# Spectral layer and feed-forward on one core: new places for pairs, chunks and waves in the slot plan, y in two slots, the sum split a slot later, parts of the inverse matrices kept in DRAM

## The chip, the core and the metric

The program runs on one core of one Trainium2 chip. The metric is device time in microseconds, from the first to the last instruction of the program; lower is better. The engines that matter are TensorE (PE in the profile; its weight loads are PEld), VectorE (DVE), ScalarE (ACT), GpSimd (POOL) and SyncE (SP), which issues the DMAs.

## The reference

```python
X = np.fft.rfft(x, axis=1)                     # x: 8 x 3008 x 256, float32
Yr = Xr @ w_r - Xi @ w_i + b_r
Yi = Xr @ w_i + Xi @ w_r + b_i
Y  = sign(Y) * max(abs(Y) - 0.01, 0)           # both parts
y  = np.fft.irfft(Y, n=3008, axis=1)
h  = y.reshape(24064, 256) @ w_in              # 256 x 2048
out = (h - np.tanh(h)) @ w_out                 # 2048 x 256
```

## The kernel before

**The feed-forward and its slots.** The 24064 tokens are cut into 48 chunks of some 502, and the 2048 inner columns into 16 blocks of 128; one block of one chunk is a *slot*, so there are 768 slots, and 16 slots are a *band*. In slot g, TensorE first does the six "up" matmuls (L691, into h) of slot g+2, then what the plan has put into slot g, then the six "down" matmuls (L724, into the two banks o) of slot g. Each product is three matmuls, because both operands are split into a high and a low part: g = h - tanh(h) is made by ACT (th, L702) and DVE (g, L705), and split by ACT (gh, L708) and DVE (gl, L711). At a band's end ACT (L734) and DVE (L742) copy the two banks o to ot, and the next band's first "down" needs these banks.

**The spectral work in between.** The length 3008 = 64 x 47 is transformed in two steps, forward and backward, batch by batch. Batch 0 is done ahead of the slots, in an order written out by hand. For batches 1 to 7 the work lies in the slots:

- a *fold* (class Folded): DVE adds and subtracts inputs (L333), TensorE does 32 small matmuls in one go (L342) into **four** banks of PSUM's pool ps_f, and ACT and DVE write the result to the DRAM tensor a; four per batch (two for batch 1)
- a *pair* (class Both, two units of class Spectrum): 64 small matmuls (L494) into **two** banks of ps_f; `take` copies and splits the result on ACT and DVE (xh, xl, xi), and splits the sum xi (s)
- the unit's products: `cross` (L419, bank ps_v of ps_f, held until DVE has added y, L450) and `shared` (L419, bank ps_t of ps_f; DVE: tb L436, y L450 four times, mn L439 and L440)
- `matrix`: loads the unit's inverse matrix (turn) and splits it (turn_h on ACT, turn_l on DVE); `inverse` (L465 to L467, a bank ps_i of ps_f, copied to zo by ACT, L472), which is stored to the DRAM tensor z
- a *wave* (class Wave): 80 small matmuls (L654) into **two** banks of ps_f, in two halves that use different rows of the array; the results are copied to yt by ACT and DVE (L663) and split by `halves` into yh and yl, the chunk's input

**What sets the order.** Pool ps_f has four banks, and fold, pair, wave, ps_v, ps_t and ps_i share them. `plan_spectrum`, `plan_folded` and the loop over chunks put each step into a numbered slot (`put`); the instructions are then written slot by slot, and the framework's scheduler may still shift an instruction within its engine by a little. Each engine then runs its own queue strictly in that order. The plan before puts a wave into the slot of a pair, where one is near:

```python
near = range(asked[w] + 6, min(asked[w] + 11, last + 1))
slot = asked[w] + 3 if c == 2 else next((k for k in near if k in whole), near[len(near) // 2])
```

Of the kernel before, what the change touches and what calls it, by code (L numbers as in the profile page):

```python
# [10 lines left out]
F32 = mybir.dt.float32  # L11
# [3 lines left out]
ALU = mybir.AluOpType  # L15

B, S, D, FF = 8, 3008, 256, 2048
NP, NJ, KR, GB = 32, 24, 48, 5
# [77 lines left out]
def spectral_ffn(ctx, tc, x, w_r, w_i, w_in, w_out, x_fold, b_turned, f1, f1b, f1f, f2, f2f, i1, i1w, i2, out):  # L96
    nc = tc.nc
    P = 128
# [34 lines left out]
    def split(src, name, pool=const, tag=None, bufs=None, rest=nc.vector):  # L133
        hi, lo = pair_like(src, name, pool, tag, bufs)
        split_into(hi, lo, src, rest)
        return hi, lo
# [113 lines left out]
            nc.gpsimd.tensor_tensor(out=lo, in0=self.w, in1=hi.bitcast(F32), op=ALU.subtract)  # L250

    a_dram, z_dram = {}, {}
    XC = 4
    PAIRED, LOOK = 1, 4
    NEAR = 32
# [119 lines left out]
    class Spectrum:  # L375
# [20 lines left out]
        def take(self, ps):  # L396
            self.xh = work.tile([P, 2, 2, P], F32R, name="xh", tag="sp_h", bufs=3)
            self.xl = work.tile([P, 2, 2, P], F32R, name="xl", tag="sp_l", bufs=3)
            xi = work.tile([P, 2, P], F32, name="xi")
            flat, one = "p t r (j s k) -> p s (t r j) k", "p t (j s k) -> p s t j k"  # L400
            xh, xl = (x.rearrange(flat, j=2, s=2) for x in (self.xh, self.xl))
            xv = xi.rearrange(one, j=2, s=2)
            whole = [p.rearrange("p (x k) -> p x k", k=32) for p in ps]
            part = [p.rearrange("p (t r j k) -> p r t j k", t=2, r=2, j=2) for p in ps]
            for s in range(2):
                nc.scalar.copy(out=xh[:, s], in_=whole[s])  # L406
            for s in range(2):
                nc.scalar.copy(out=xv[:, s], in_=part[s][:, 1])
            for s in range(2):
                nc.vector.tensor_tensor(out=xl[:, s], in0=whole[s], in1=xh[:, s].bitcast(F32), op=ALU.subtract)  # L410
            for s in range(2):
                nc.vector.tensor_tensor(out=xv[:, s], in0=part[s][:, 0], in1=xv[:, s], op=ALU.add)  # L412
            self.s = split(xi, f"s_{self.b}_{self.jp}", work, "s")

        def product(self, dst, hi, lo, w):
            n = 0
# [10 lines left out]
                self.product(self.vv[:, D:], self.xh[:, :, 0], self.xl[:, :, 0], lin[1])  # L427

        def matrix(self):
            self.turns = split(self.turn, f"turn_{self.b}_{self.jp}", work, "turn", 2)  # L430

        def shared(self):
            t1 = ps_f.tile([P, 512], F32, name="ps_t1", tag="f")
            self.product(t1[:, :D], *self.s, lin[0])
            tb = self.temp("tb", "th")
            nc.vector.tensor_tensor(out=tb, in0=t1[:, :D].unsqueeze(1).to_broadcast([P, 2, D]), in1=bias, op=ALU.add)  # L436
            y = self.add(lambda jj, ri: tb[jj * 64:(jj + 1) * 64, ri, :])
            mn = work.tile([P, 2, D], F32, name="mn", tag="tmp", bufs=4)
            nc.vector.tensor_scalar_min(out=mn, in0=y, scalar1=-LAM)  # L439
            nc.vector.scalar_tensor_tensor(out=mn, in0=y, scalar=LAM, in1=mn, op0=ALU.max, op1=ALU.add)  # L440
            self.mn = mn
# [1 line left out]
        def halve(self):  # L443
            self.z = split(self.mn, f"z_{self.b}_{self.jp}", work, "sp", 3)

        def add(self, common):
            y = self.temp("y", "g")
            for ri in range(2):
                for jj in range(2):
                    nc.vector.tensor_tensor(  # L450
                        out=y[ri * 64:(ri + 1) * 64, jj, :], in0=common(jj, ri),
                        in1=self.side(ri)[jj * 64:(jj + 1) * 64], op=ALU.add,
                    )
            return y

        def side(self, ri):
            return self.vv[:, ri * D:(ri + 1) * D]
# [12 lines left out]
        def put(self, pz):  # L470
            zo = work.tile([P, 512], F32, name="zo", tag="tmp", bufs=4)
            nc.scalar.copy(out=zo, in_=pz)  # L472
            self.zo = zo
            self.store(0, P)
# [28 lines left out]
    class WholeSpectrum(Spectrum):  # L503
# [22 lines left out]
        def sum(self):  # L526
            pr = self.ps.rearrange("p (t r m) -> p t r m", t=2, r=2)
            self.sf = work.tile([P, 2, P], F32, name="sf", tag="s_h")
            nc.vector.tensor_tensor(out=self.sf, in0=pr[:, :, 0, :], in1=self.xf[:, :, 1, :], op=ALU.add)
# [28 lines left out]
        def common(self):  # L558
            self.tb = work.tile([P, D], F32, name="tb0", tag="xi")
            nc.scalar.copy(out=self.tb, in_=self.t1)  # L560
# [62 lines left out]
    class Wave:  # L623
# [20 lines left out]
        def time(self):  # L644
            half = self.half
            ps = [ps_f.tile([P, 512], F32, name="ps_i2", tag="f") for _ in range(2)]
            pv = [p[:, :2 * half * 47].rearrange("p (t c) -> p t c", t=2) for p in ps]
            for k in range(half):
                for t in range(2):
                    for h in range(2):  # L650
                        rows = slice(64 * h, 64 * h + KR)
                        for c in range(2):
                            at = t * P + 64 * c
                            nc.tensor.matmul(  # L654
                                pv[h][64 * c:64 * c + 64, t, 47 * k:47 * k + 47],
                                self.zt[rows, k, at:at + 64], i2t[rows, :47], start=True, stop=True,
                            )
            pool, tag = self.home
            for t in range(2):
                self.y[t] = pool.tile([P, PITCH], F32, name="yt", tag=tag)  # L660
            for h, copy in enumerate((nc.scalar.copy, nc.vector.tensor_copy)):
                for t in range(2):
                    copy(out=self.y[t][:, 47 * h * half:47 * (h + 1) * half], in_=pv[h][:, t])  # L663

# [327 lines left out]
    def put(slot, fn, *a, turn=1):  # L992
        slots.setdefault(slot, ([], [], []))[turn].append((fn, a))

    def plan_folded(b, wanted):
        last = 0
        for k, ideal in enumerate(wanted):
            f = Folded(b, k)
            spots = [g for g in range(max(last + 6, ideal - 4), ideal + 9) if all(abs(g - h) > 2 - (b == 2) for h in busy) and g not in held]
            at = min(spots, key=lambda g: abs(g - ideal) + 2 * (g % NF > 10))  # L1000
            put(max(FIXED, at - 6, last + 1), f.load)
            for i in range(4):
                put(max(FIXED, at - 4 + i), f.fold, i // 2, i % 2)
            put(at, f.dft, turn=2)
            for g in range(2):
                put(at + 1 + g, f.join, g, turn=0)
            last = at

    def plan_spectrum(units, start, each, ahead, lag, rest):
        for jp, s in enumerate(units):  # L1010
            at = start + int(jp * each)
            early = start + int((jp - jp % 2) * each)
            put(early - ahead, s.load)
            if jp % 2:
                pair = Both(units[jp - 1:jp + 1])
                put(early, pair.dft, turn=2)
                for v in range(2):
                    put(early + v, pair.take, v, turn=0 if v else 2)
                whole.add(early)
            if units is not second or jp >= 2:  # L1020
                put(at + lag - 3, s.load_turn)
                put(at + lag, s.matrix)
            put(at + lag, s.cross, 0)
            held.update((at + lag, at + lag + 1))
            put(at + lag + 1, s.cross, 1)
            put(at + lag + 2, s.shared)
            put(at + lag + 2 + rest, s.halve)
            put(at + 2 * lag + 3 + rest // 2, s.inverse)

    put(FIXED, load_second)  # L1030
    whole, held = set(), set()
    asked, new = {}, {}
    for c in range(2, NCH):
        new[c] = [w for w in chunks[c].parts if w.w > 1 and w not in asked]
        last, spaced = (9, 1) if c == 2 else (2, 4)
        for k, w in enumerate(reversed(new[c])):
            asked[w] = NF * (c - 1) + last - spaced * k
    plan_spectrum(second, 46, 2.95, 5, 2, 0)
    asked[waves[len(waves) // B]] += 4
    ends = {b: asked[waves[b * len(waves) // B]] - 2 for b in range(2, B)}  # L1040
    for b in range(2, B):
        plan_spectrum([Spectrum(b, jp) for jp in range(NJ // 2)], ends[b] - 61, 4.6, 5, 2, 2)
    busy = set(whole)
    for c in range(2, NCH):
        last = NF * (c - 1) + 12
        for w in new[c]:
            put(asked[w], w.load)
            near = range(asked[w] + 6, min(asked[w] + 11, last + 1))
            slot = asked[w] + 3 if c == 2 else next((k for k in near if k in whole), near[len(near) // 2])
            put(slot, w.time, turn=2)  # L1050
            busy.add(slot)
        for t in range(2):
            put(min(slot + 1 + t, last + 1), chunks[c].halves, t)
    plan_folded(1, (33, 39))
    plan_folded(2, (73, 79, 85, 96))
    for b in range(3, B):
        plan_folded(b, range(ends[b] - 106, ends[b] - 70, 9))
    for g in range(FIXED, len(order)):
        if g + AHEAD < len(order):
            c, f = order[g + AHEAD]  # L1060
# [50 lines left out]
```

## Time and profile before

| | |
|---|---|
| runs | 2483.96, 2479.15, 2486.25 us; median 2483.96 |
| the profiled execution | 2483.84 us, of which its span is 2482.1 us |
| mean granted TensorE clock | 0.997 |
| TensorE busy | 2460.8 us, 99% of the span |
| VectorE, ScalarE busy | 1827.0 us (74%), 1344.8 us (54%) |
| DMA | 182.73 MB, the main queue busy 25.4% of 16 engines' span |

The profiled execution lies 0.12 us under the median. A busy TensorE here does not say that it runs at its peak: matmuls overlap, and their ends are modelled. What it loses is read from the distance of the *starts* of its instructions in the timeline.

### The profile page before, as it was taken

To read this page: it belongs to the slowest core of one execution; us is meant where nothing else is said; L and a number is where in the kernel's file an instruction comes from. 1 tells how busy PE (TensorE), PEld (TensorE's weight loads), DVE (VectorE), ACT (ScalarE), POOL (GpSimd) and SP (SyncE) were. 2 spreads that over 40 slices of the span, in tenths; PEclk is the share of its full clock that TensorE was granted. 3 is DMA by queue.
4 is the path that set the end of the run, shared out by engine and by line. 5 is a ranking of instruction groups with operands and counts; after the bars stand their busy time and mean duration, and the time that the engine had idled before them with its cause. 6 is when DMAs were issued, how large, how long until landed. Compare 5 with 4: busy or idle time off the path is not lost.

```text
span 2482.1 us, 47486 instructions
## 1 busy us (share of the span) xinstructions
PE 2460.8 (99%) x19274; PEld 2147.9 (87%) x19274; DVE 1827.0 (74%) x3421; ACT 1344.8 (54%) x2755; POOL 34.5 (1%) x31
## 2 busy tenths in 40 slices
PE   9999999999999999999999999999999999999999
PEld 6798978888888898888888888889888898888888
DVE  5887887677777777777776778767786687755555
ACT  5665555555555555555555555555455555554554
POOL 2110000000000000000000000000000000000000
PEclk9999999999999999999999999999999999999999
DMA  8633134111341114311143212421124221010000
GB/s 259 184 88 109 65 97 127 46 58 47 103 105 41 63 39 112 97 56 55 39 127 81 65 51 58 114 76 53 51 65 98 59 60 44 31 50 17 24 14 17
DMA packets 121323, 182.73 MB, mean 74 GB/s; under 512 B 11985, under 2 KB 85807, under 8 KB 121104
## 3 DMA queue, kind: packets, MB, share of 16 engines
q1 hardware_dynamic: 121104, 179.70, 25.4%
q8 instruction: 151, 2.47, 0.4%
q14 instruction: 68, 0.56, 0.1%
HBM read 104.68 MB, written 74.97 MB: 72 GB/s over the span
## 4 chain that ended last, share of the span: by engine, by line
PE 88%; DVE 7%; ACT 3%; DMA 1%; issue 1%; SPq 0%; ACTq 0%; DVEq 0%
PE o L724 37%; PE h L691 36%; PE ps_v L419 4%; PE ps_i L654 3%; PE ps_t L419 2%; PE ps_f L494 1%; DVE g L705 1%; DVE y L450 1%; PE ps_f L342 1%; DVE gl L711 1%; PE ps_f L290 1%; PE ps_i L465 1%; PE ps_i L466 1%; PE ps_i L467 1%; ACT gh L708 1%
## 5 line engine op out<-in xcount | busy, mean ns | idle before, releaser
L708 ACT CAST gh<-g 128x502 fp32r<-128x502 f32 (+2 forms) x768 | 469.4, 611 | 547.5 <-DVE g L705 545.1
L711 DVE TENSOR_TENSOR gl<-g,gh 128x502 fp32r<-128x502 f32 (+2 forms) x768 | 522.0, 680 | 298.4 <-ACT gh L708 286.6
L705 DVE TENSOR_TENSOR g<-h,th 128x502 f32<-128x502 f32 (+2 forms) x768 | 520.5, 678 | 261.0 <-ACT th L702 256.6
L702 ACT ACTIVATE th<-h 128x502 f32<-128x502 f32 (+2 forms) x768 | 453.3, 590 | 441.8 <-PE h L691 437.8
L724 PE MATMUL o<-gh,wout_l 128*128 128x502 f32 (+2 forms) x1536 | 590.7, 385 | 3.5 <-ACT ot L734 2.9
L724 PE MATMUL o<-gl,wout_h 128*128 128x502 f32 (+2 forms) x1536 | 577.6, 376 | 0.0
L724 PE MATMUL o<-gh,wout_h 128*128 128x502 f32 (+2 forms) x1536 | 577.3, 376 | 0.0
L691 PE MATMUL h<-yh,win_l 128*128 128x502 f32 (+2 forms) x1536 | 452.6, 376 | 2.1 <-DVE g L705 1.3
L691 PE MATMUL h<-yl,win_h 128*128 128x502 f32 (+2 forms) x1536 | 451.6, 376 | 0.7 <-DVE yl L683 0.7
L691 PE MATMUL h<-yh,win_h 128*128 128x502 f32 (+2 forms) x1536 | 451.3, 376 | 0.0
L724 PEld LDWEIGHTS o<-gh,wout_l 128*128 128x128 f32 x1536 | 290.4, 189 | 63.4 <-ACT th L702 13.4
L691 PEld LDWEIGHTS h<-yh,win_l 128*128 128x128 f32 x1536 | 289.8, 189 | 40.0 <-DVE g L705 2.1
L691 PEld LDWEIGHTS h<-yl,win_h 128*128 128x128 f32 x1536 | 290.7, 189 | 36.7 <-DVE yl L683 2.2
L724 PEld LDWEIGHTS o<-gl,wout_h 128*128 128x128 f32 x1536 | 290.5, 189 | 36.6 <-DVE gl L711 1.2
L691 PEld LDWEIGHTS h<-yh,win_h 128*128 128x128 f32 x1536 | 291.1, 190 | 34.7
L724 PEld LDWEIGHTS o<-gh,wout_h 128*128 128x128 f32 x1536 | 290.9, 189 | 27.6 <-issue 0.8
L450 DVE TENSOR_TENSOR y<-tb,ps_v 64x256 f32<-64x256 f32 x336 | 140.1, 417 | 3.4
L682 ACT CAST yh<-yt 128x470 fp32r<-128x470 f32 (+38 forms) x200 | 83.0, 460 | 24.5 <-PE h L691 15.9
L683 DVE TENSOR_TENSOR yl<-yt,yh 128x470 fp32r<-128x470 f32 (+38 forms) x200 | 78.5, 420 | 16.1 <-ACT yh L682 14.8
L654 PEld LDWEIGHTS ps_i<-i,zin 48*64 48x64 f32 x4096 | 72.6, 137 | 19.5 <-issue 11.9
L654 PE MATMUL ps_i<-i,zin 48*64 48x47 f32 x4096 | 79.7, 235 | 3.7 <-DVE w_f L245 1.5
L406 ACT CAST xh<-ps_f 128x256 fp32r<-128x256 f32 x168 | 58.8, 374 | 43.0 <-DVE xi L412 42.8
(116 smaller groups left out, 2210.5 us busy)
## 6 DMA issues: line engine op xcount, KB each, us to landing
xt<-in_x_fold SPq DMA_DIRECT2D x52, 512.0 KB
at<-a SPq DMA_DIRECT2D x96, 256.0 KB
z<-zo SPq DMA_DIRECT2D x92, 256.0 KB
zin<-z SPq DMA_DIRECT2D x92, 240.0 KB
a<-st SPq DMA_DIRECT2D x216, 96.0 KB
out<-ot SPq DMA_DIRECT2D x29, 502.0 KB
turn<-in_i SPq DMA_DIRECT2D x84, 128.0 KB
out<-ot SPq DMA_DIRECT2D x16, 504.0 KB
```

The source lines that it names most:

```text
L406: nc.scalar.copy(out=xh[:, s], in_=whole[s])
L419: nc.tensor.matmul(paired(dst, D), lhs[:, t], in_turn(rhs[:, t, :]), start=n == 0, stop=n == 5)
L450: nc.vector.tensor_tensor(out=y[ri * 64:(ri + 1) * 64, jj, :], in0=common(jj, ri), in1=self.side(ri)[jj * 64:(jj + 1) * 64], op=ALU.add,)
L654: nc.tensor.matmul(pv[h][64 * c:64 * c + 64, t, 47 * k:47 * k + 47], self.zt[rows, k, at:at + 64], i2t[rows, :47], start=True, stop=True,)
L682: nc.scalar.copy(out=yh, in_=y)
L683: nc.vector.tensor_tensor(out=yl, in0=y, in1=yh.bitcast(F32), op=ALU.subtract)
L691: nc.tensor.matmul(paired(h, n), lhs[:, t, f * P:(f + 1) * P], moving(rhs[:, t], n), start=k == 0, stop=k == 5,)
L702: nc.scalar.activation(out=th[:, :n], in_=h[:, :n], func=AF.Tanh)
L705: nc.vector.tensor_tensor(out=g[:, :n], in0=h[:, :n], in1=th[:, :n], op=ALU.subtract)
L708: nc.scalar.copy(out=gh[:, :n], in_=g[:, :n])
L711: nc.vector.tensor_tensor(out=gl[:, :n], in0=g[:, :n], in1=gh[:, :n].bitcast(F32), op=ALU.subtract)
L724: nc.tensor.matmul(paired(self.o[t], n), lhs[:, f, t * P:(t + 1) * P], in_turn(rhs[:, :n]), start=f == 0 and k == 0, stop=f == NF - 1 and ...
```

## The change

All places are now chosen by new rules. A pair is moved off the last two slots of a band (`clear`) and planned together with its two units (`plan_pair`); a wave goes, within its five slots, to the one farthest from pairs, folds and other waves; a fold is kept out of the slots from a unit's products to its threshold (`held`) and pays for each slot that it is nearer than 3 to another burst. For batches 2 to 7 y is added in two slots instead of one. The split of the sum is a step of its own, a slot later than `take`. The split inverse matrices of batch 1 are written to DRAM, and batches 2 to 7 load both parts from there, into the tiles that the splits wrote before. For all batches but 0, ACT makes all four copies yt of a wave. The arithmetic is the same, and so is the number of TensorE's instructions of each kind.

```diff
 def take(self, ps):
...
-            self.s = split(xi, f"s_{self.b}_{self.jp}", work, "s")
+            self.xi = xi
+
+        def sum(self):
+            self.s = split(self.xi, f"s_{self.b}_{self.jp}", work, "s")
...
         def matrix(self):
+            if self.b > PAIRED:
+                self.turns = pair_like(i1[:, :2], f"turn_{self.b}_{self.jp}", work, "turn", 2)
+                for k, t in enumerate(self.turns):
+                    nc.sync.dma_start(out=t.bitcast(F32), in_=turns_dram[self.jp, k])
+                return
             self.turns = split(self.turn, f"turn_{self.b}_{self.jp}", work, "turn", 2)
+            for k, t in enumerate(self.turns):
+                nc.sync.dma_start(out=turns_dram[self.jp, k], in_=t.bitcast(F32))
...
-            for h, copy in enumerate((nc.scalar.copy, nc.vector.tensor_copy)):
+            for h in range(2):
+                copy = nc.scalar.copy if h == 0 or self.b else nc.vector.tensor_copy
...
+    def away(g):
+        return min(abs(g - h) for h in busy)
...
-            spots = [g for g in range(max(last + 6, ideal - 4), ideal + 9) if all(abs(g - h) > 2 - (b == 2) for h in busy) and g not in held]
-            at = min(spots, key=lambda g: abs(g - ideal) + 2 * (g % NF > 10))
+            spots = [g for g in range(max(last + 6, ideal - 4), ideal + 9) if g not in held]
+            at = min(spots, key=lambda g: abs(g - ideal) + 2 * (g % NF > 10) + 5 * max(0, 3 - away(g)))
...
+    def plan_pair(units, at, apart, calm):
+        pair = Both(units)
+        put(at, pair.dft, turn=2)
+        busy.add(at)
+        for v, s in enumerate(units):
+            put(at - 5, s.load)
+            put(at + v, pair.take, v, turn=0 if v else 2)
+            put(at + 1 + v, s.sum)
+            g = at + v * apart + 2
+            if s.b > PAIRED or s.jp >= 2:
+                if s.b == PAIRED:
+                    put(g - 3, s.load_turn)
+                put(g, s.matrix)
+            for k in range(2):
+                put(g + k, s.cross, k)
+            held.update(range(g, g + 2 + 2 * calm))
+            put(g + 2, s.shared)
+            put(g + 2 + calm, s.threshold)
+            put(g + 2 + 2 * calm, s.halve)
+            put(g + 5 + calm, s.inverse)
+
+    def clear(g):
+        while g % NF in (14, 15):
+            g += 1 if g % NF == 15 else -1
+        return g
...
-            slot = asked[w] + 3 if c == 2 else next((k for k in near if k in whole), near[len(near) // 2])
+            slot = asked[w] + 3 if c == 2 else max(near, key=lambda g: min(4, away(g)))
```

**Where it shows in the order: a fold.** TensorE's queue, first fold of the batch that starts near slot 166; `ps_t` is the unit's last product, `ps_f...<-e` the fold. Before:

```order
L419 MATMUL ps_t_7588<-w_h,s_10_h 128x256 x2
L724 MATMUL o_7377<-gh,wout_l 128x502
L724 MATMUL o_7377<-gh,wout_h 128x502
L724 MATMUL o_7377<-gl,wout_h 128x502
L724 MATMUL o_7378<-gh,wout_l 128x502
L724 MATMUL o_7378<-gh,wout_h 128x502
L724 MATMUL o_7378<-gl,wout_h 128x502
L691 MATMUL h<-yh,win_l 128x502 x2
L691 MATMUL h<-yh,win_h 128x502 x2
L691 MATMUL h<-yl,win_h 128x502 x2
L342 MATMUL ps_f_7629<-e,f1f 32x512
L342 MATMUL ps_f_7630<-e,f1f 32x512
```

In the changed kernel the same fold stands in slot 173, four slots behind the last product, and right behind that unit's inverse (`ps_i`):

```order
L705 MATMUL h<-yh,win_l 128x502 x2
L705 MATMUL h<-yh,win_h 128x502 x2
L705 MATMUL h<-yl,win_h 128x502 x2
L478 MATMUL ps_i_7861<-z_11_l,turn_11_h 128x256
L479 MATMUL ps_i_7861<-z_11_h,turn_11_l 128x256
L480 MATMUL ps_i_7861<-z_11_h,turn_11_h 128x256
L478 MATMUL ps_i_7861<-z_11_l,turn_11_h 128x256
L479 MATMUL ps_i_7861<-z_11_h,turn_11_l 128x256
L480 MATMUL ps_i_7861<-z_11_h,turn_11_h 128x256
L343 MATMUL ps_f_7873<-e,f1f 32x512
L343 MATMUL ps_f_7874<-e,f1f 32x512
```

The fold moved from one slot behind a product to four slots behind it, and an inverse moved in front of it.

**A wave.** TensorE's queue in slot 522 before: the end of a pair (`ps_f...<-...at`), then the wave (`ps_i...<-...zin`), cut in two by the scheduler:

```order
L494 MATMUL ps_f_20997<-f_135,at 64x2x32 x2
L494 MATMUL ps_f_20998<-f_135,at 64x2x32 x2
L654 MATMUL ps_i_21046<-i_259,zin 64x47 x20
L724 MATMUL o_20614<-gh,wout_l 128x504
L724 MATMUL o_20614<-gh,wout_h 128x504
L654 MATMUL ps_i_21047<-i_259,zin 64x47 x20
L724 MATMUL o_20614<-gl,wout_h 128x504
L724 MATMUL o_20615<-gh,wout_l 128x504
```

A wave of the changed kernel, in slot 508; the nearest pair stands four slots ahead, in slot 504, and the wave follows an inverse and a unit's last product:

```order
L480 MATMUL ps_i_20308<-z_1_h,turn_1_h 128x256
L423 MATMUL ps_t_20318<-w_h,s_2_l 128x256 x2
L423 MATMUL ps_t_20318<-w_l,s_2_h 128x256 x2
L423 MATMUL ps_t_20318<-w_h,s_2_h 128x256 x2
L667 MATMUL ps_i_20334<-i_260,zin 64x47 x2
L667 MATMUL ps_i_20335<-i_260,zin 64x47 x2
L667 MATMUL ps_i_20334<-i_260,zin 64x47 x2
```

Pair and wave moved apart, the wave is whole, and its two halves alternate again; an inverse and a product stand in front of it instead.

**A band's end.** DVE's queue at the end of the band in front of slot 160 in the changed kernel (at the same band end before, `ot` stands ahead of `tb` and of all four `y`):

```order
L719 TENSOR_TENSOR g<-h,th 128x502
L447 TENSOR_TENSOR tb<-ps_t_7333,bias 128x512
L725 TENSOR_TENSOR gl<-g,gh 128x502
L465 TENSOR_TENSOR y<-tb,ps_v 64x256 x2
L756 COPY ot<-o_6730 128x504
L465 TENSOR_TENSOR y<-tb,ps_v 64x256 x2
L719 TENSOR_TENSOR g<-h,th 128x502
```

Here tb and two of the y moved in front of the copy ot.

## Rows read from the trace of the kernel before

**Rows 1.** Timeline of PE: a fold alone; columns: start us, length us, instruction.
```profile
666.39 0.63 PE L342 MATMUL ps_f<-e,f1f 24*32 24x512 f32 x4
...
667.46 0.48 PE L724 MATMUL o<-gh,wout_l 128*128 128x502 f32 x1
667.77 0.38 PE L724 MATMUL o<-gh,wout_h 128*128 128x502 f32 x1
667.99 0.38 PE L724 MATMUL o<-gl,wout_h 128*128 128x502 f32 x1
```

**Rows 2.** Timeline of PE: a fold one slot behind a product; in brackets: idle, releaser.
```profile
1842.10 1.05 PE L342 MATMUL ps_f<-e,f1f 24*32 24x512 f32 x6
1843.41 0.61 PE L342 MATMUL ps_f<-e,f1f 24*32 24x512 f32 x1 [0.25 <-DVE y L450]
...
1844.47 0.48 PE L724 MATMUL o<-gh,wout_l 128*128 128x502 f32 x1
```

**Rows 3.** Timeline of all engines: a fold right behind an inverse.
```profile
377.46 1.36 PE L342 MATMUL ps_f<-e,f1f 24*32 24x512 f32 x7
377.57 0.59 ACT L472 COPY zo<-ps_i 128x512 f32<-128x512 f32 x1
...
379.27 0.48 PE L724 MATMUL o<-gh,wout_l 128*128 128x502 f32 x1
```

**Rows 4.** Timeline of PE: a fold cut in two around three "down" matmuls.
```profile
327.06 1.47 PE L342 MATMUL ps_f<-e,f1f 24*32 24x512 f32 x5
...
331.45 0.48 PE L724 MATMUL o<-gh,wout_l 128*128 128x502 f32 x1
```

**Rows 5.** Timeline of PE: a wave alone, a pair alone, a pair with a wave.
```profile
425.53 1.38 PE L654 MATMUL ps_i<-i,zin 48*64 48x47 f32 x80
426.84 0.48 PE L724 MATMUL o<-gh,wout_l 128*128 128x504 f32 x1
...
461.66 1.16 PE L494 MATMUL ps_f<-f,at 64*64 64x64 f32 x64
462.75 0.48 PE L724 MATMUL o<-gh,wout_l 128*128 128x502 f32 x1
...
490.52 1.16 PE L494 MATMUL ps_f<-f,at 64*64 64x64 f32 x64
...
492.78 0.48 PE L724 MATMUL o<-gh,wout_l 128*128 128x502 f32 x1
```

**Rows 6.** Timeline of PE: product, pair and a wave cut in two, around two "downs".
```profile
1451.58 1.16 PE L494 MATMUL ps_f<-f,at 64*64 64x64 f32 x64
1453.03 1.37 PE L654 MATMUL ps_i<-i,zin 48*64 48x47 f32 x40 [0.29 <-DVE tb L436]
...
1456.72 0.48 PE L724 MATMUL o<-gl,wout_h 128*128 128x504 f32 x1
```

**Rows 7.** Busy time by stretch: us, PE, PEld, DVE, ACT, POOL, granted clock, DMA, GB/s.
```profile
1758.90:1766.00 7.10, 7.05 (x52) 6.04 (x53) 3.99 (x12) 2.15 (x8) 0.00 (x0) 0.52 0.10 30
...
2066.40:2069.80 3.40, 3.40 (x14) 2.73 (x11) 2.79 (x9) 1.80 (x6) 0.00 (x0) 0.50 0.22 58
```

**Rows 8.** Timeline of PE: first "down" matmuls of a band, at two band ends.
```profile
559.71 0.39 PE L419 MATMUL ps_v<-w_h,xh 128*128 128x256 f32 x2
561.05 0.48 PE L724 MATMUL o<-gh,wout_l 128*128 128x504 f32 x1 [0.96 <-ACT ot L734]
...
1626.33 0.48 PE L724 MATMUL o<-gh,wout_l 128*128 128x502 f32 x1 [0.22 <-DVE ot L742]
```

**Rows 9.** Timeline of PE: first "up" matmuls of a chunk whose wave came late.
```profile
1103.74 0.69 PE L691 MATMUL h<-yl,win_h 128*128 128x504 f32 x2 [0.49 <-DVE yl L683]
```

**Rows 10.** Groups by line: count, then busy us, mean ns, idle before and releaser.
```profile
L143 DVE TENSOR_TENSOR turn_l<-turn,turn_h 128x256 fp32r<-128x256 f32 x84 | 36.2, 431 | 7.5 <-ACT turn_h L142 7.1
L663 ACT COPY yt<-ps_i 128x235 f32<-128x235 f32 (+1 forms) x112 | 32.4, 341 | 3.3 <-PE ps_i L654 3.2
```

**Rows 11.** The chain that ended last: start us, us, what; the slowest landing in it.
```profile
969.94 6.58 DMA xt<-in_x_fold
```

More of the change, by code (lines that the diff above doesn't have):

```diff
@@ L252, in spectral_ffn @@
     a_dram, z_dram = {}, {}
+    turns_dram = dram.tile([NJ // 2, 2, P, 2, P], F32, name="turns", bufs=1)
     XC = 4
@@ L434, in shared, with threshold @@
             self.product(t1[:, :D], *self.s, lin[0])
-            tb = self.temp("tb", "th")
+            tb = self.tb = self.temp("tb", "th")
             nc.vector.tensor_tensor(out=tb, in0=t1[:, :D].unsqueeze(1).to_broadcast([P, 2, D]), in1=bias, op=ALU.add)
-            y = self.add(lambda jj, ri: tb[jj * 64:(jj + 1) * 64, ri, :])
+            self.y = self.temp("y", "g")
+            self.add(0)
+        def threshold(self):
+            y = self.y
+            self.add(1)
             mn = work.tile([P, 2, D], F32, name="mn", tag="tmp", bufs=4)
@@ L444, in halve, with add @@
             self.z = split(self.mn, f"z_{self.b}_{self.jp}", work, "sp", 3)
[L446 to L454, printed above, removed]
+        def add(self, ri):
+            for jj in range(2):
+                rows = slice(jj * 64, jj * 64 + 64)
+                nc.vector.tensor_tensor(
+                    out=self.y[ri * 64:(ri + 1) * 64, jj, :], in0=self.tb[rows, ri, :], in1=self.side(ri)[rows], op=ALU.add,
+                )
         def side(self, ri):
@@ L1006, in plan_folded @@
                 put(at + 1 + g, f.join, g, turn=0)
+            busy.add(at)
             last = at
[L1009 to L1028, printed above, removed]
+    def plan_pair(units, at, apart, calm):
+        pair = Both(units)
+        put(at, pair.dft, turn=2)
+        busy.add(at)
+        for v, s in enumerate(units):
[18 more added lines that the diff above has]
+        return g
     put(FIXED, load_second)
-    whole, held = set(), set()
+    busy, held = set(), set()
     asked, new = {}, {}
@@ L1037, in spectral_ffn @@
             asked[w] = NF * (c - 1) + last - spaced * k
-    plan_spectrum(second, 46, 2.95, 5, 2, 0)
+    for jp in range(0, NJ // 2, 2):
+        plan_pair(second[jp:jp + 2], 46 + int(jp * 2.95), 3, False)
     asked[waves[len(waves) // B]] += 4
@@ L1041, in spectral_ffn @@
     for b in range(2, B):
-        plan_spectrum([Spectrum(b, jp) for jp in range(NJ // 2)], ends[b] - 61, 4.6, 5, 2, 2)
-    busy = set(whole)
+        units = [Spectrum(b, jp) for jp in range(NJ // 2)]
+        for jp in range(0, NJ // 2, 2):
+            plan_pair(units[jp:jp + 2], clear(ends[b] - 61 + int(jp * 4.6)), 4, True)
+    busy |= {27, 28}
+    plan_folded(1, (33, 39))
+    plan_folded(2, (84, 90, 97, 103))
+    for b in range(3, B):
+        plan_folded(b, range(ends[b] - 99, ends[b] - 72, 8))
     for c in range(2, NCH):
@@ L1053, in spectral_ffn @@
             put(min(slot + 1 + t, last + 1), chunks[c].halves, t)
[L1054 to L1057, printed above, removed]
     for g in range(FIXED, len(order)):
```

## The prediction

> **What bounds the kernel now.** The first part of the page has TensorE busy almost throughout, so I looked for what TensorE does in that time, in the timeline of PE. In a slot without extra work a matmul starts every 0.21 us [rows 1], 12 of them make 2.54 us, and a burst of small matmuls stands between "up" and "down" at a price of its own: 1.07 us for a fold (666.39 to 667.46), 1.09 for a pair, 1.31 for a wave [rows 1, 5]. Leaving a burst costs 0.10 us more (the first "down" takes 0.31 instead of 0.21 [rows 1]); entering one costs the same, so 0.20 together. Most slots of the trace run at exactly these prices. VectorE and ScalarE have room on average, so only places count where TensorE's starts are farther apart. I went through all slots for such places, and then asked the chain of waits and the brackets of the timeline who ended each wait. Nearly all of them are waits for a PSUM bank, or bursts that got in each other's way. So the gain can be no more than the sum of these places, and each is asked: is it still there in the new order?
>
> **The change part by part.**
>
> *Folds.* A fold needs all four banks of ps_f. Before there are 26. Of these 17 cost 1.07 us. Four stand one slot behind a product, and wait until DVE has added y and so released ps_v: 1842.10 to 1844.47, 2.37 us, 1.30 too much [rows 2]. Two stand right behind an inverse and wait for the copy zo: 1.81 us, 0.74 too much [rows 3]. Three stand in the slot of the product itself, and the scheduler cut them in two: 4.39 us from 327.06 to 331.45, less three "downs" (0.64) and the 1.07: 2.68 too much [rows 4]; I take 2.68 for all three. Sum 5.2 + 1.5 + 8.0 = 14.7 us. In the new order none is cut, none stands nearer than two slots behind a product (a slot is 2.54 us, more than the 1.30 that is late now), but four stand right behind an inverse, as in [rows 3]: 4 x 0.74 = 3.0 stays. **-11.7 us.**
>
> *Pairs and waves.* Before, 11 waves follow a pair in its slot. Six are whole: 490.52 to 492.78, 2.26 us, where pair and wave alone cost 1.09 + 1.31 + 0.20 = 2.60; moving them apart costs 6 x 0.34 = 2.0. Three stand behind a product and a pair, and find no bank: the wave waits for tb, then for y, is cut in two, and each half takes as long as a whole wave (1.30), since its two halves no longer alternate. 1451.58 to 1456.72 is 5.14 us, less two "downs" (0.42): 4.72, 2.12 too much [rows 6], times three 6.4. Two more are cut in batch 1, one of their halves without a wait; half the price, 1.06 each. In the new order no wave is cut or follows a pair. -(6.4 + 2.1 - 2.0) = **-6.5 us.**
>
> *Clock.* Behind two of the three cut waves the granted clock falls to 1.2 GHz: 0.52 over 7.1 us and 0.50 over 3.4 us [rows 7], that is 7.1 x 0.48 + 3.4 x 0.50 = 5.1 us lost. Just before, TensorE had done a pair and a cut wave with three waits. Elsewhere, delayed folds included, the clock is 1.00. As this pattern is gone: **-5.1 us.**
>
> *New neighbours.* In nine slots a pair (six) or a wave (three) now follows an inverse and a product, with a bank to wait for that zo's copy releases. In [rows 3] the bank comes 0.74 us late to a burst right behind the inverse; here a product lies between, six matmuls of half the columns, 6 x 0.11 = 0.67 us. Bounds 0 and 0.74 each; I take 0.1, nearest to the covered case: **+0.9 us** (at most 6.7).
>
> *Band ends.* Before, three band ends with a product and `take` at the same place wait for ACT's copy ot: due 0.22 us after 559.71, come at 561.05, 1.12 late, 3.4 in all; eleven more are late by 0.1 to 0.5 us, as at 1626.33 (0.22 in the bracket, and 0.16 that the modelled end of the matmul before hides, as in the other one: 1.12 against 0.96) [rows 8], some 3.3 in all. New: `clear` moves pairs away, but four band ends have a fold's additions ahead of DVE's copy, as that one, three have tb and two y ahead of it (some 1.7 us, at 0.43 for 256 columns on DVE [rows 10]), one has tb and four, and the ones with xl and xi stay similar. I take 0.4 for each of the first eight and 0.25 for seven others, 5.0 instead of 6.7: **-1.7 us** (bounds -6.7, and +3 if the new ones cost as much as the old worst).
>
> *Late waves.* Before, at three chunk starts the "up" matmuls wait for yh and yl, since the wave stood behind a pair late in the band: the bracket has 0.49 us for the worst wait [rows 9]; with the shorter ones at the same starts some 0.9 each, 2.7. In the new order waves of such a kind are earlier, or whole and alone; three late ones behind a product stay, with yl fewer instructions back in DVE's queue; 0.3 each. **-1.8 us.**
>
> *Inverse matrices and yt.* 72 splits leave DVE (0.431 us, 31 us in all) and ACT (about as much), and 98 copies yt move to ACT (0.341 us, 33 us) [rows 10]. No wait of TensorE is put down to them, so they are worth 0 on the path beyond the places above. DMA grows by 72 x 128 KB of loads and 24 x 128 KB of stores: 0, hidden, since a load has six slots, over 15 us, until its inverse, and the slowest landing in the chain took 6.58 us [rows 11]. If that cover were gone, see the first rival. y in two slots holds ps_v a slot longer; in the new order nobody asks for that bank in this slot. The later split of the sum puts four products of batch 1 (before two) into the middle of the "down" matmuls, and waits that an order can't show will come: **+2.5 us** (0 to 6).
>
> Sum: -11.7 - 6.5 - 5.1 + 0.9 - 1.7 - 1.8 + 2.5 = -23.4. From the profiled execution, 2483.84: **2460.4 us**; the median of the runs lies 0.12 above, so 2460.
>
> **A rule that speaks against it.** The Trainium skill (TensorEngine Tiling (Array Packing), section Tiling Modes) says that changing the tiling mode, not just the tile, drains TensorE. Fold, pair and wave use parts of the array, so each burst on its own pays two such changes; the new order has more bursts of their own. The trace agrees with 0.10 us on either side [rows 1]. The page gives no price; by the rows it is inside the 2.0 us of the six whole couples.
>
> **The rivals.**
>
> *Slower: the loads come late.* Turn matrices now come on SP's queue, behind stores that wait for data. If a load landed after its inverse should start, TensorE would stand still 72 times. The point from which it decides: about 16 us from issue to landing, against 6.58 as the slowest in the chain; each 0.5 us beyond costs 36 us, and 31 us are wanted to be slower by over 0.3%: 2491 or more. Chance 0.04.
>
> *No change: ACT late behind four copies.* A wave's four copies now hold ACT for 4 x 0.34 = 1.4 us before the next tanh. Between the end of an "up" and the "up" that needs its bank again lie 3.8 us (three groups of six); tanh and g, passes like the copy zo's 0.59 us [rows 3], take 1.2. With 1.4 us more it still fits; if DVE's queue adds over 1 us at each of some 40 waves, 0.5 us would be lost at each, 20 us: 2480. Against it: DVE loses 64 us of work. Chance 0.06.
>
> *The clock falls elsewhere.* Six batches with one fall each of 7 us would cost 6 x 3.4 = 20 us: 2481. Against it: lone bursts, and even 2.37 us for a delayed fold, leave it at 1.00. The Trainium skill (TensorE: Matmul & The Clock Gate, section "A second HAM failure mode: psum-queue depth-cycling") describes a kernel whose clock swings because TensorE pauses often while it goes through PSUM banks, and the new order has more single bursts; the trace shows such falls only behind [rows 6]' pattern. Chance 0.05.
>
> *Half.* New collisions for banks and band ends give back 10 us or more: only the cuts and the clock stay won, 2470 to 2474. Chance 0.15. It speaks for it that the order shows where a bank is taken, but not when.
>
> **Numbers.** My forecast (2450 to 2470) has 0.70. 0.3% is 7.5 us, about what a measurement of this kernel can tell from no change; faster than 2476.5: forecast and half, and a part of the others, 0.88; within 0.3%: 0.08; slower: 0.04. Range: if band ends and late waves vanish altogether and nothing new comes, 2483.8 - 14.7 - 6.5 - 5.1 - 6.7 - 2.7 = 2448; if the nine new neighbours cost 0.74 each, the band ends stay as they are and 6 us come new, 2471, and some more for half. 8 in 10: **2452 to 2474.**
>
> **What would show it.** In the new timeline: folds of 1.07 us, four of 1.81; no wave in two pieces; the granted clock at 1.00 after the start; fewer waits for y at fold and wave; the DMA landing of the turn tiles well ahead of the inverse. Wrong it would be through a wait for these tiles, tanh late behind yt, or a new fall of the clock.

## The result, and the profile after

The changed kernel takes **2455.11 us** (median of four runs, 2453.82 to 2457.06), before 2482.26 in the same job: ratio 0.989, 95% interval [0.9873, 0.9908]. The forecast was 2460, range 2452 to 2474. The profiled execution is one of 2457.06 us, with a span of 2455.3.

The page's busy times, and from its chain the shares by engine (before: PE 88%, DVE 7%, ACT 3%):

```profile
PE 2439.8 (99%) x19274; PEld 2139.6 (87%) x19274; DVE 1781.7 (73%) x3251; ACT 1346.0 (55%) x2781; POOL 34.5 (1%) x31
PE 93%; DVE 3%; DMA 2%; ACT 1%; issue 0%; SPq 0%; ACTq 0%; DVEq 0%
```

TensorE still fills the span, and the chain runs through it more than before; VectorE is busy 45 us less. The table by stretch (us, PE, PEld, DVE, ACT, POOL, granted clock, DMA, GB/s) answers to [rows 7]:

```profile
94.50:101.30 6.80, 6.80 (x107) 5.32 (x100) 4.40 (x9) 4.35 (x10) 1.27 (x2) 0.50 0.80 269
101.30:2453.00 2351.70, 2345.01 (x18685) 2070.38 (x18683) 1719.14 (x3140) 1285.94 (x2665) 10.35 (x8) 1.00 0.26 73
```

From 101.3 us to the last matmul the clock is at 2.4 GHz; the falls of [rows 7] are not in this execution. The stretch at half speed ahead of it, in batch 0, is in the trace of before too.

TensorE's timeline, at a pair, a fold, a band end and two waves:

```profile
543.18 0.33 PE L507 MATMUL ps_f<-f,at 64*64 64x64 f32 x4
543.76 1.15 PE L507 MATMUL ps_f<-f,at 64*64 64x64 f32 x60 [0.24 <-ACT zo L485]
544.84 0.48 PE L738 MATMUL o<-gh,wout_l 128*128 128x502 f32 x1
...
648.19 1.36 PE L343 MATMUL ps_f<-e,f1f 24*32 24x512 f32 x7
...
650.00 0.48 PE L738 MATMUL o<-gh,wout_l 128*128 128x502 f32 x1
...
959.21 0.38 PE L738 MATMUL o<-gl,wout_h 128*128 128x504 f32 x1
961.69 0.48 PE L738 MATMUL o<-gh,wout_l 128*128 128x504 f32 x1 [2.10 <-DVE ot L756]
...
1692.08 1.44 PE L667 MATMUL ps_i<-i,zin 48*64 48x47 f32 x80
1693.45 0.48 PE L738 MATMUL o<-gh,wout_l 128*128 128x502 f32 x1
...
1732.21 1.38 PE L667 MATMUL ps_i<-i,zin 48*64 48x47 f32 x80
1733.53 0.48 PE L738 MATMUL o<-gh,wout_l 128*128 128x504 f32 x1
```

The fold behind an inverse takes 1.81 us (648.19 to 650.00), as in [rows 3]; there are four. A pair behind inverse and product takes 1.66 instead of the 1.09 of [rows 5], since the copy zo holds its second bank; there are three of these, and three more with 0.06. No wave is cut. The one that stood cut in two in slot 522, as in [rows 6], is now in slot 520, whole, and takes 1.32 (1732.21 to 1733.53). The wave of slot 508, whose order stands above next to that of slot 522, is another one: before, it stood whole behind the pair of slot 504; now it takes 1.37, behind an inverse and a product. The band end at 959.21 is new and the worst place of the kernel: 2.48 us between two starts instead of 0.21. VectorE's rows and then SP's say why:

```profile
955.94 0.68 DVE L725 TENSOR_TENSOR gl<-g,gh 128x504 fp32r<-128x504 f32 x1 [0.68 <-ACT gh L722]
959.16 1.29 DVE L334 TENSOR_TENSOR e<-xt 128x512 f32<-128x512 f32 x2 [2.54 <-DMA xt<-in_x_fold]
960.37 0.67 DVE L719 TENSOR_TENSOR g<-h,th 128x504 f32<-128x504 f32 x1
960.96 0.67 DVE L756 COPY ot<-o 128x502 f32<-128x502 f32 x1
```

```profile
950.07 0.53 SPq L490 DMA_DIRECT2D z<-zo  x1
954.51 0.32 SPq L655 DMA_DIRECT2D zin<-z  x1
954.88 0.44 SPq L328 DMA_DIRECT2D xt<-in_x_fold  x1
```

VectorE waits 2.54 us for a fold's inputs, with ot in its queue behind. Their load was issued only at 954.88, because the load zin ahead of it on SP's queue waits (3.8 us by the waits of SP) until the store z has landed.

For the whole kernel I took each group of TensorE's instructions (an "up", a burst, a "down") from its first start to the next one's, less its price from the prediction, and added up all that is over 0.05 us, from slot 26 on. Before, that is 41.1 us, after 10.8: less 30.3. Taking six whole pair-and-wave couples apart costs 2.0, so 28.3 are to be seen; the two profiled executions differ by 26.8, of which 0.6 is a later start of slot 26. I call these the *losses* of a kernel below. They come from one profiled execution each; what happens ahead of slot 26 is not in them.

### The profile page after: what moved, and what is told of

It is laid out like the page before. It is cut to its first block, busy times and chain, and to the rows that moved or that the text cites. A ratio compares the mean times of both kernels' runs of the same rounds, so it can differ in the third digit from the quotient of the medians.

```text
span 2455.3 us, 47509 instructions
## 1 busy us (share of the span) xinstructions
PE 2439.8 (99%) x19274; PEld 2139.6 (87%) x19274; DVE 1781.7 (73%) x3251; ACT 1346.0 (55%) x2781; POOL 34.5 (1%) x31
## 4 chain that ended last, share of the span: by engine, by line
PE 93%; DVE 3%; DMA 2%; ACT 1%; issue 0%; SPq 0%; ACTq 0%; DVEq 0%
PE o L738 39%; PE h L705 38%; PE ps_v L423 4%; PE ps_i L667 3%; PE ps_t L423 2%; PE ps_f L507 2%; PE ps_f L343 1%; PE ps_i L480 1%; PE ps_i L479 1%; PE ps_i L478 1%; DVE g L719 1%; DMA a<-st 1%; PE ps_f L291 0%; DVE gl L725 0%; DVE w_s L242 0%
## 5 line engine op out<-in xcount | busy, mean ns | idle before, releaser
L411 DVE TENSOR_TENSOR xl<-ps_f,xh 128x256 fp32r<-128x256 f32 x168 | 64.1, 419 | 24.6 <-ACT xi L409 23.3
L667 PEld LDWEIGHTS ps_i<-i,zin 48*64 48x64 f32 x4096 | 66.3, 136 | 16.2 <-issue 11.9
```

Of the source, the lines that this page charges most:

```text
L667: nc.tensor.matmul(pv[h][64 * c:64 * c + 64, t, 47 * k:47 * k + 47], self.zt[rows, k, at:at + 64], i2t[rows, :47], start=True, stop=True,)
```

## The experiments

Ratios are to the kernel before, measured in the same job (its medians there: 2482.78, 2482.73 and 2484.73 us in the three jobs).

**Which part of the change? `places_alone`, `rest_alone`, `waves_alone`, `folds_alone`.** The first takes only the changed kernel's plan (`clear`, `away`, `held`); the second everything else and the old plan. The other two are the kernel before with one rule each:

```diff
 # waves_alone
+            if slot in whole:
+                slot = max(near, key=lambda g: min(4, min(abs(g - h) for h in whole)))
 # folds_alone
-            held.update((at + lag, at + lag + 1))
+            held.update(range(at + lag, at + lag + 2 + 2 * (rest > 0)))
```

> The changed kernel with its new places for pairs, folds and waves, but with everything else as before: inverse matrices split in every batch, half of yt on DVE, y in one slot, the sum split with take. Theory 'places' (the gain comes from bursts on TensorE that no longer wait for a PSUM bank, are not cut, and don't let the clock fall): 2455 to 2463 us, the clock at 1.00 after the start, no wave or fold in two pieces. Rival 'relief' (the gain comes from 64 us less work on DVE, which shortens all waits): most of the gain is gone, 2470 us or more.

> The kernel before with its old places, and the rest of the change: inverse matrices from DRAM, all yt of batches 1 to 7 on ACT, y in two slots, the sum split a slot later. Theory 'places': 2474 to 2486 us, folds of 2.4 us and cut waves as before. Rival 'relief': 2455 to 2468 us.

> The kernel before, in which only the waves that shared a slot with a pair are moved away from the pairs; folds and pairs stay where they were. Theory 'places': the cut waves cost 8.5 us, moving the six whole couples apart costs 2.0, the clock gives 5.1, and waves that came late behind a pair some 2.7: about -14 us, 2464 to 2472 us, and the clock at 1.00 after the start. If the clock falls for another reason: it falls again, 2471 to 2477. Rival 'relief': 2478 us or more.

> The kernel before, in which only the folds are kept out of the slots from a unit's products to its threshold; waves and pairs stay where they were. Four delayed folds (1.30 us each) and one cut fold (2.7) go, two more folds stand behind an inverse (0.74 each). Theory 'places': -6.4 us, 2473 to 2478 us; the falls of the clock stay. Rival 'relief': 2480 us or more.

Measured: places alone 2455.46 us, 0.9888 [0.9874, 0.9901], with losses of 11.5 us: the whole gain. Its slot 26 starts 2.4 us earlier than the changed kernel's, as its early stretch at half speed is missing; from there to the end the two profiled executions differ by 0.5 us. The rest alone: 2481.11, 0.9989 [0.998, 0.9998], losses 40.0. The three band ends that waited for ACT's copy ot ([rows 8], 1.12 each) still lose 1.16 each; now VectorE's copy is the late one, as TensorE's timeline shows for the first:

```profile
563.93 0.38 PE L705 MATMUL h<-yh,win_h 128*128 128x504 f32 x1
565.30 0.48 PE L738 MATMUL o<-gh,wout_l 128*128 128x504 f32 x1 [0.99 <-DVE ot L756]
```

The three chunk starts with a late wave lose 2.2 to 2.3 us each instead of 0.7 to 1.3, 4.1 more in all. The clock did not fall behind any of the three cut waves here; behind two of them it did in the trace of before, which cost 5.1 us. By the medians the rest alone is worth 1.7 us, of some 27. Waves alone: 2470.08, 0.9948 [0.9934, 0.9962], losses 24.3, and in the profiled execution (2468.13, the fastest of five; the slowest took 2475.38) the clock holds, with all folds as late and as cut as before:

```profile
6.00:2466.00 2460.00, 2442.47 (x19268) 2135.72 (x19267) 1824.30 (x3416) 1340.17 (x2754) 29.39 (x22) 1.00 0.26 74
```

Folds alone 2480.07, 0.9985 [0.9976, 0.9993]: less than the 5 to 10 us expected, and at the edge of what the rival 'relief' had forecast. But the trace shows the folds' gain, and where it went. (Beside the line shown, this kernel gives a fold four more slots to choose from.) The folds lost 6.1 us less, as they should, but the moved folds put their additions ahead of ot at band ends. TensorE's and VectorE's timelines at one of them:

```profile
1272.25 0.38 PE L724 MATMUL o<-gl,wout_h 128*128 128x504 f32 x1
1274.44 0.48 PE L724 MATMUL o<-gh,wout_l 128*128 128x504 f32 x1 [1.82 <-DVE ot L742]
```

```profile
1271.91 1.29 DVE L333 TENSOR_TENSOR e<-xt 128x512 f32<-128x512 f32 x2 [2.26 <-DMA xt<-in_x_fold]
1273.13 0.68 DVE L705 TENSOR_TENSOR g<-h,th 128x504 f32<-128x504 f32 x1
1273.72 0.67 DVE L742 COPY ot<-o 128x502 f32<-128x502 f32 x1
```

That is the same kind of stall as the one at 959.21 of the changed kernel; the losses of the "down" groups are 3.5 us higher than before (15.3 against 11.8), so more than half of the folds' gain went there. The clock fell as often as before, behind two of the three cut waves (3.4 and 6.8 us).

**Waves back. `waves_back`** is the changed kernel with the old rule for a wave's slot.

> The changed kernel, but a wave goes again into the slot of a pair where one is near: 11 waves follow a pair in its slot, 2 of them are cut in two by the scheduler (before the change five were cut), everything else as in the changed kernel. Theory 'places': the whole couples cost 0.34 us less than apart (9 x 0.34 = 3.1 us won), each cut wave costs 1.1 to 2.1 us, a wait for a bank of a product ahead of the couple 0.3 to 1 us where there is one, and chunk starts behind late waves some 0.3 us each: 2454 to 2460 us at full clock. If the clock falls behind a cut wave as before the change, 1.7 to 3.4 us for each fall more: up to 2466 us. Rival 'a wave near a pair is harmless, the gain came from VectorE's lighter load': 2452 us, three below the changed kernel, with no new waits.

Measured: 2471.14 us, 0.9951 [0.9936, 0.9967]: some 16 us over the changed kernel, far above what was expected. Losses 28.8. TensorE's timeline in slot 408, VectorE's y there, and the clock behind three such slots:

```profile
1384.61 0.39 PE L423 MATMUL ps_t<-w_h,s_l 128*128 128x256 f32 x2
...
1385.38 1.17 PE L507 MATMUL ps_f<-f,at 64*64 64x64 f32 x62
...
1386.40 1.03 PE L667 MATMUL ps_i<-i,zin 48*64 48x47 f32 x28
1388.55 1.37 PE L667 MATMUL ps_i<-i,zin 48*64 48x47 f32 x50 [1.11 <-DVE y L465]
1389.84 0.48 PE L738 MATMUL o<-gh,wout_l 128*128 128x502 f32 x1
```

```profile
1386.79 1.71 DVE L465 TENSOR_TENSOR y<-tb,ps_v 64x256 f32<-64x256 f32 x4
```

```profile
1390.70:1394.20 3.50, 3.50 (x11) 2.78 (x10) 2.25 (x8) 1.94 (x8) 0.00 (x0) 0.51 0.56 140
1692.00:1696.00 4.00, 4.00 (x59) 3.62 (x56) 3.30 (x13) 3.43 (x13) 0.00 (x0) 1.00 0.57 155
1994.90:1998.30 3.40, 3.40 (x10) 2.70 (x9) 2.58 (x8) 2.28 (x10) 0.00 (x0) 0.50 0.69 148
```

The wave isn't cut by "downs" here, but its second half waits until y has released ps_v: 3.44 us instead of 1.3, three times (slots 408, 504 and 600). It is the meeting of [rows 6], product, pair and wave in one slot, in new slots: before, it stood in 426, 522 and 618; the pairs' new places moved the product into the slots of the other couples. The two slots of y have no part in it: the four y stand right behind each other, and the last one ends 3.88 us behind the start of the product's first matmul in these three slots, and 3.88 too in the same slots of `y_sum_back` (below), where y is added in one. The clock falls behind two of the three. And at three chunk starts the "up" matmuls wait for yh and yl of a late wave: 2.3 us each, where the kernel before lost 0.7 to 1.3 [rows 9]. `rest_alone` loses 2.2 to 2.3 there with the old places, so this price belongs to the rest of the change, and the new places hide it. Which part of the rest it is was not tested; ACT's four copies yt, which stand ahead of yh in its queue, are the nearest guess.

**The stalls that are left. `load_early`, `inverse_apart`, `inverse_apart_load_early`, `zin_other_queue`.**

```diff
 # load_early
-            put(max(FIXED, at - 6, last + 1), f.load)
+            put(max(FIXED, at - 7, last + 1), f.load)
 # inverse_apart (starts: the slots of the batch's pairs)
-            put(g + 5 + calm, s.inverse)
+            back = g + 5 + calm
+            back += back in starts
+            held.add(back)
+            put(back, s.inverse)
 # zin_other_queue, Wave.load_part
-                nc.sync.dma_start(out=self.zt[...
+                nc.gpsimd.dma_start(out=self.zt[...
```

> The changed kernel with one number changed: a fold's inputs xt are loaded seven slots ahead of it instead of six. Theory 'load order' (the 2.37 us that TensorE waits at 958.8 us come from xt, issued on SP's queue only at 954.88 us, since SP stood waiting with a store ahead of it; VectorE then waits 2.54 us for xt with ot behind it): this one wait goes or falls below 0.5 us, everything else stays; 2452 to 2454 us, ratio to the changed kernel 0.9990. Rival 'VectorE is simply full at this band end': the wait stays at 1 to 2.4 us whenever xt lands, 2455 us. A third way: the earlier load waits for a free tile of xt and holds SP's queue longer, so that other loads come late: 2456 us or more.

> The changed kernel with one more rule: an inverse that would fall into the slot where a pair starts goes a slot later, and a fold keeps out of the slots with an inverse. No fold and no pair then stands behind an inverse (three waves still do). Theory 'the copy zo holds the bank' (four folds 0.74 us late each, three pairs about 0.48, three about 0.06): 2.9 + 1.6 = 4.5 us go, 2449 to 2452 us, ratio to the changed kernel 0.998. Rival 'it is the burst's length that counts': folds and pairs stay as late as they are, 2455 us. Second rival: the moved folds and inverses meet band ends and VectorE's queue, and give 2 to 5 us back: 2453 to 2456 us.

> Both edits together: inverses apart from pairs and folds, and xt loaded seven slots ahead. If both theories hold and are independent, 4.5 + 2.0 = 6.5 us go: 2447 to 2450 us, ratio to the changed kernel 0.9974. If the waits are only exchanged for others, 2453 to 2456 us.

> The changed kernel with the loads zin of the waves issued by GpSimd instead of SP; TensorE's order is the same to the row. Theory 'head of the queue' (at the band end of slot 272 the load xt stands on SP's queue behind a zin load that waits 3.8 us until the store z has landed, so xt is issued at 954.88 us instead of about 950.6, VectorE waits 2.54 us for it, and the copy ot stands behind VectorE): xt is issued right behind the store z, VectorE finds it there, and the 2.37 us of TensorE fall below 0.4; all other stalls stay: 2452.5 to 2453.5 us, ratio to the changed kernel 0.9992. Rival 'landing, not issue' (xt takes over 6 us to land next to the other loads): the stall stays over 1 us, 2455 us. Second rival: GpSimd's loads come later than SP's and the waves wait for zin: 2457 us or more.

Inverses apart: 2449.72 us, 0.9866 [0.9848, 0.9884], losses 4.6 instead of 10.8; of the folds one of 1.78 us is left, no pair is late. That is more than the 4.5 us expected: the stall of slot 272 is gone too, and slots 240 and 336 lose 0.6 each instead. The fold of slot 173 has moved, stands behind an "up", and takes its 1.07 (643.38 to 644.45):

```profile
643.38 0.63 PE L343 MATMUL ps_f<-e,f1f 24*32 24x512 f32 x4
...
644.45 0.48 PE L738 MATMUL o<-gh,wout_l 128*128 128x502 f32 x1
```

The stall of slot 272 went because the fold ahead of it moved a slot forward, too: xt is then issued at 944.61 us, ahead of the store z (950.71) and the load zin. The early load alone gives 2453.61, 0.9883 [0.9865, 0.9901]. That is the time expected, but the stall that should have gone is still there, with 1.64: in SP's queue the load xt stands behind the same zin load at slot 272 (it needs the tile that the fold before releases). Both edits: **2448.91 us, 0.9862 [0.9847, 0.9878]**, the fastest kernel of the study, losses 3.8; its interval overlaps that of inverses apart.

The zin loads on GpSimd's queue make the test that the early load didn't. SP's and VectorE's timelines around the same band end, and VectorE's at a later place:

```profile
957.70 0.53 SPq L490 DMA_DIRECT2D z<-zo  x1
958.89 0.34 SPq L328 DMA_DIRECT2D xt<-in_x_fold  x1
```

```profile
963.23 1.29 DVE L334 TENSOR_TENSOR e<-xt 128x512 f32<-128x512 f32 x2 [0.35 <-DMA xt<-in_x_fold]
...
1279.38 1.29 DVE L334 TENSOR_TENSOR e<-xt 128x512 f32<-128x512 f32 x2 [4.71 <-DMA a<-st]
```

xt is issued 1.2 us behind the store z instead of 4.8, VectorE waits 0.35, and TensorE's stalls of slots 272 and 176 are gone: the cause is the head of SP's queue. The kernel as a whole is slower, 2464.25, 0.9928 [0.9913, 0.9942], against my expectation and in the range of its second rival: slot 26 starts 7 us later, and the scheduler put a fold's additions earlier into VectorE's queue, where they wait 4.71 us, by the chain for the stores of st (eight of them on SP, 3.2 us more until they land). TensorE stands for it, and the clock falls behind it:

```profile
1281.32 0.79 PE L738 MATMUL o<-gl,wout_h 128*128 128x504 f32 x1 [3.06 <-DVE gl L725]
```

```profile
1281.20:1284.70 3.50, 3.38 (x8) 2.80 (x9) 3.14 (x6) 1.35 (x3) 0.00 (x0) 0.51 0.19 30
```

Of the later start TensorE's timeline shows one part, a wait of batch 0's waves for zin (in the changed kernel these waves start at 93.14):

```profile
97.31 4.93 PE L667 MATMUL ps_i<-i,zin 48*64 48x47 f32 x160 [2.74 <-DMA zin<-z]
```

Another part is 13.7 us at half speed in batch 0 instead of 6.8. Why the clock stays low for longer is open.

**What the rest is for. `copies_back`, `y_sum_back`, `places_apart`.** The first two undo a part of the changed kernel; the third is places alone with the two edits of the fastest kernel.

```diff
 # copies_back, Wave.time; and matrix() splits in each batch
-            for h in range(2):
-                copy = nc.scalar.copy if h == 0 or self.b else nc.vector.tensor_copy
+            for h, copy in enumerate((nc.scalar.copy, nc.vector.tensor_copy)):
 # y_sum_back
-            put(at + 1 + v, s.sum)
+            put(at + v, s.sum, turn=0 if v else 2)
-            put(g + 2 + calm, s.threshold)
+            put(g + 2, s.threshold)
```

> The changed kernel with the splits of the inverse matrices made anew in each batch (no copy in DRAM) and half of the copies yt on VectorE again; TensorE's order is the same to the row. Theory 'off the path' (my term of 0): 2454 to 2456 us; the stall of slot 272 may be some 1 us shorter, since no loads of split matrices stand on SP's queue there, as with the new places alone (1.13 us). Rival 'VectorE's 64 us count': stalls for ot, y and yl at band ends and waves, 2458 us or more. Rival 'ACT late behind four copies' (the other way round): 2452 us or less.

> The changed kernel with y added in one slot and the sum split in take's slot again. My term for these was +2.5 us (0 to 6), for a few waits in batch 1 between slots 53 and 80, where the changed kernel shows 1.5 us in all; undone, 2453 to 2455 us. Theory 'they help at places of their own' (with the old places the three waits of 1.12 us for ot at band ends went away with them): 2456 to 2459 us. If the two slots of y keep ps_v a slot longer at a cost: 2452 us or less.

> The kernel with the new places alone (splits of the inverse matrices, yt, y and the sum as before the change), with inverses apart from pairs and folds, and xt loaded seven slots ahead. Theory 'places are all': the same time as the changed kernel with these two edits, 2447 to 2451 us. Rival 'VectorE's lighter load is needed once TensorE waits less' (VectorE does 64 us more in this kernel): new waits for ot, yl or y, 2453 us or more.

Measured: copies back 2458.0 us, 0.99 [0.9884, 0.9916], losses 12.3; y and sum back 2457.58, 0.9903 [0.9884, 0.9922], losses 12.8. By the medians they lie 2.9 and 2.5 us over the changed kernel, by the losses 1.5 and 2.0, and the intervals overlap: neither theory nor rival is decided by the times. (That three waits of 1.12 us went away with y and sum, as one expectation says, is a misreading: `rest_alone` only exchanged the copy that is late.) The traces show what for: without the copies kept away from VectorE, ot is 0.27 to 0.41 late at six more band ends (slots 144, 160 and each 96 on), while the stall of slot 272 gets 1.0 shorter; with y in one slot the band ends at 160, 256 and 352 lose 0.5 instead of nothing. Places apart: 2452.5, 0.988 [0.9864, 0.9896], 3.6 over the fastest and between the two ranges expected. VectorE's and TensorE's timelines where it loses 1.34, three times:

```profile
555.07 0.69 DVE L143 TENSOR_TENSOR z_l<-mn,z_h 128x512 fp32r<-128x512 f32 x1
555.69 0.68 DVE L716 TENSOR_TENSOR gl<-g,gh 128x504 fp32r<-128x504 f32 x1
556.29 0.42 DVE L143 TENSOR_TENSOR turn_l<-turn,turn_h 128x256 fp32r<-128x256 f32 x1
556.63 0.68 DVE L747 COPY ot<-o 128x502 f32<-128x502 f32 x1
```

```profile
557.36 0.48 PE L729 MATMUL o<-gh,wout_l 128*128 128x504 f32 x1 [1.07 <-DVE ot L747]
```

In the fastest kernel this band end loses 0.05 and the other two 0.6 each. So the rest of the change was worth nothing in the changed kernel that the runs could tell from zero, and perhaps 3.6 us once the inverses had moved: by the traces 4.1 of losses, 2.7 of it at these three band ends, where a split turn_l that the rest removes stands ahead of ot. The intervals of these two kernels overlap, so the times alone don't show it.

## Why the prediction was right, and where its terms were off

- **Places, not load.** That the gain comes from TensorE's late starts, and that the new places remove them, is shown by `places_alone` and `rest_alone`.
- **Folds.** None is cut or behind a product by less than two slots. I left 3.0 us for four; it is 3.65, with a fifth that waits for VectorE's xt. That the copy zo holds their bank is shown by `inverse_apart`.
- **Pairs, waves, clock.** 13.4 us forecast with the late waves; `waves_alone` measures 12.7 (2482.78 to 2470.08). The late waves left nothing, where I had left 0.9. For the clock, the runs correct the reason I gave for rejecting its rival: I wrote that it falls only behind cut waves. In `waves_back` it fell behind two of three whole waves with one wait, in `zin_other_queue` behind the wait of 3.4 us at 1281, and in `rest_alone` behind a fold cut in two (358.06 to 359.05, then 3.4 us at half speed), but behind none of the three cut waves. So the -5.1 is what one execution of the kernel before lost, and that the new order keeps the clock up is seen, not explained. What decides within such a pattern is open.
- **New neighbours.** The term was mis-sized: +0.9 forecast (0.1 each), 2.0 measured. Three pairs cost 0.53 to 0.56 each, near the upper bound, three pairs and three waves 0.06. I thought that the product between covers the copy zo. In the three dear places ACT has a late yh and a tanh in its queue ahead of zo, as ACT's timeline of the changed kernel shows for the first; the inverse ends at 542.4:

```profile
541.53 1.22 ACT L696 CAST yh<-yt 128x396 fp32r<-128x396 f32 x2 [0.78 <-PE h L705]
542.65 0.59 ACT L716 ACTIVATE th<-h 128x502 f32<-128x502 f32 x1
543.13 0.57 ACT L485 COPY zo<-ps_i 128x512 f32<-128x512 f32 x1
...
1677.31 0.58 ACT L485 COPY zo<-ps_i 128x512 f32<-128x512 f32 x1
```

  At 1677, where zo follows at once on the inverse's end (1677.1), the pair loses 0.06.
- **Band ends.** 5.0 us forecast as left, 4.1 measured (with the two of batch 1), but not where I put them: fifteen small ones became 2.37 at slot 272, 0.53, 0.48 and 0.47, and two of 0.1. I read VectorE's order there and priced a fold's additions as work (0.4); their wait for a load stood on SP's queue, where I had not looked. It is the rival of the late loads, at one place and with another load: `zin_other_queue` shows it.
- **Inverse matrices, yt: 0.** Right within what the runs can tell; no wait is put down to the loaded tiles. But at slot 272 the new loads seem to cost something: in `copies_back` and `places_alone`, which don't have them, the load zin is issued 2.8 and 2.4 us behind the store z instead of 4.4, and the stall of 2.37 is 1.42 and 1.13. No run takes out the loads alone.
- **Later sum, y in two slots and unseen: +2.5.** 1.1 us show up, in batch 1 (slots 53 to 76). The later sum is not their cause: in `y_sum_back` the same places are late, and some more so (0.26 at slots 70 and 76 instead of 0.08, 0.65 at slot 64 instead of 0.48). And y in two slots hardly holds ps_v longer: in 68 of 72 units the last y ends at the same time behind the product as in `y_sum_back`, within 0.01 us.
- **Sum.** I had left 12.3 us in all (3.0, 0.9, 5.0, 0.9 and 2.5), and there are 10.8 (3.65, 2.0, 4.1, 0 and 1.1). The profiled execution is 3.3 below the 2460.4 of the sum: 1.5 are that, 1.8 are not assigned. The median lies another 1.95 below the profiled execution. That the sum came so near is in part luck: a stall of 2.37 us that was not foreseen stands where smaller ones had been forecast.

## What to carry to other kernels

Where one engine is full and its neighbours have room, price the starts that come late, and move the work that meets: a burst that wants a bank should not stand in the slot of the one that gives it back. When additions for a later step stand ahead of a copy that the full engine waits for, read the queue of the load that they need as well, since one waiting load holds up all behind it. Relief of an engine that isn't the bound may show nothing while other waits stand in front of it; it is worth another try when they are gone, though the runs here don't settle that.

## What was not expected of the hardware

The granted clock falls for 3.4 or 6.8 us behind some waits and not behind others of the same kind: of three equal slots of `waves_back` (3.44 us each), two fell to 0.51 and 0.50 and one stayed at 1.00; of the three cut waves in slots 426, 522 and 618 the clock fell behind the last two in the trace of before, behind the first two in `folds_alone`, and behind none in `rest_alone`; the wait of 2.48 us at slot 272 of the changed kernel left it at 1.00, the one of 3.4 us in `zin_other_queue` did not. The early stretch at half speed, 6.8 us in the traces before and after, was missing in three other executions (`places_alone`, `waves_alone`, `y_sum_back`).
